# Earlier token transfers, later first weights, and transposing a chunk ahead in a retention and gated-projection kernel

## The chip, the cores and the metric

The kernel runs on one core of one Trainium2 chip. The metric is the device time of one execution in microseconds (us), as the median of several runs. The span of a trace is about 1.8 us shorter than the device time of the same run. All runs told here are of one state, the fast one. TensorE is PE in the profile, VectorE is DVE, ScalarE is ACT, GpSimd is POOL, and SyncE, which issues most transfers, is SP.

## The reference, cut to what matters

A retention block (a linear recurrence over time with a decay for each head) makes x, and x goes through two large products with a gate between them. Inputs are float32, except the two weight matrices, which are float64.

```python
# q, k, v: (4, 8, 768, 64) = batch, heads, time, head size
for t in range(S):
    state = gamma[None, :, None, None] * state + np.einsum('bhd,bhe->bhde', k[:, :, t], v[:, :, t])
    y[:, :, t] = scale * np.einsum('bhd,bhde->bhe', q[:, :, t], state)
# x = y as (3072, 512)
h = x @ w_in                                              # (3072, 2048)
sp = np.maximum(h, 0.0) + np.log1p(np.exp(-np.abs(h)))    # softplus
g = h * erf(sp)
return (g @ w_out).astype(np.float32)                     # (3072, 512)
```

## The kernel before, as far as the argument goes

The kernel takes the time axis in chunks of 128 steps. The first four chunks (0 to 3) of batch 0 make the 512 tokens of the first block. Nothing large can start before these four are through, and no large product can run before its weights are converted. This front of the kernel is what the change rearranges. For each chunk there are six steps:

- `K_` scales q and k by the decays (DVE).
- `T` transposes both on PE, and ACT copies them back.
- `S_` makes the scores on PE.
- `M` applies the causal mask and rescales (DVE).
- `O_` makes the results and the update of the state on PE, and ACT copies the results to `xT`.
- `A` adds the update to the state (DVE).

```python
    for j in range(n_first):          # the first four chunks
        S_(j)
        if j == 0:
            keep_warm(3)              # dummy matmuls
        M(j)
        if j + 1 < n_first:
            K_(j + 1)
        O_(j)
        if j + 1 < n_first:
            T(j + 1)
        ret_loads(j)                  # chunk 3 behind chunk 0; weight pieces
        pace(1)
        if j + 1 < n_first:
            A(j)
```

The weights come in 16 pieces of 1 MB. A piece is converted from float64 to float32 by integer and float operations on DVE, with one square on ACT.

```python
        nc.vector.tensor_scalar(top, hi, 3, 0x3FFFFFF8, ...)           # L205
        nc.vector.scalar_tensor_tensor(top, hi, 0xC0000000, top, ...)  # L209
        nc.scalar.activation(square, square, AF.Square)                # L213
        nc.vector.tensor_scalar(low, top, 0xFF800000, None, ...)       # L215
        nc.vector.scalar_tensor_tensor(lowf, lo, 2.0**-52, lowf, ...)  # L217
        nc.vector.tensor_tensor(lowf, topf, lowf, op=ALU.add)          # L219
        nc.vector.scalar_tensor_tensor(to, square..., lowf...)         # L221
```

These operations are not put behind one another. The build of the program deals them out between the steps of the chunks: `pace(n)` adds n to a counter called `room`, and for every whole unit one conversion operation is emitted. In the traces DVE runs its instructions in the order in which they are emitted.

## Time and profile before

| | before |
|---|---|
| median, lowest, highest of 6 runs | 715.74, 714.52, 718.07 us |
| span of the trace | 714.0 us |
| PE busy, DVE busy | 698.1 us (98%), 398.6 us (56%) |
| first matmul of the first large product | 36.43 us |
| first projection | 70.41 us |

The prediction below shows the main lines of this profile. Two more are needed. They are DVE's operations with the idle time before them in brackets, and what ended it.

```profile
15.36 1.22 DVE L397 TENSOR_TENSOR kq<-kq,kq_s 128x1024 f32<-128x1024 f32 x1 [2.35 <-DMA kq<-in_q_dram]
...
33.28 0.69 DVE L437 TENSOR_TENSOR am<-r,causal 128x512 f32<-128x512 f32 x1 [0.46 <-PE hp L425]
```

The columns are start, duration, engine, line, operation, and output and inputs. The last line is the mask of chunk 3. From there on nothing holds the first block up: its results, then the first large product 3.15 us later.

### The profile page before, as it was taken

How to read it: one execution, taken by the hardware profiler on the slowest of the kernel's cores; microseconds unless marked ns; L12 is line 12 of the kernel's file. 1: busy time of each engine (PE TensorE's matmuls, PEld its weight loads, DVE VectorE, ACT ScalarE, POOL GpSimd, SP SyncE). 2: the span in 40 equal slices, each digit the busy share in tenths (PEclk: the TensorE clock that was granted, in tenths of full speed). 3: DMA queues.
4: the chain of work that ended last, by engine and by line, in shares of the span. 5: the costliest groups of instructions: out<-in, count | busy, mean ns of one | idle time of the engine just before them, and what ended most of it. 6: DMA issues, size and time to landing. Idle time of an engine off the chain costs nothing.

```text
span 714.0 us, 12100 instructions
## 1 busy us (share of the span) xinstructions
PE 698.1 (98%) x5132; PEld 592.4 (83%) x5132; DVE 398.6 (56%) x545; ACT 256.9 (36%) x288; POOL 5.2 (1%) x18
## 2 busy tenths in 40 slices
PE   7899999999999999999999999999999999999996
PEld 6644444486999999999999999989989999999995
DVE  3899999974853553563554454544543553243323
ACT  1345653525144143243242341441441423423440
POOL 1000000010000000000000000000000000000000
PEclk9899999999999999999999999999999999999999
DMA  9999733212321232211222223220311210000000
GB/s 187 214 239 234 176 130 118 39 22 41 100 40 35 70 61 44 58 32 31 61 42 42 66 39 58 65 49 18 69 35 29 45 46 1 1 30 1 1 30 29
DMA packets 147061, 46.96 MB, mean 66 GB/s; under 512 B 135744, under 2 KB 135744, under 8 KB 147008
## 3 DMA queue, kind: packets, MB, share of 16 engines
q1 hardware_dynamic: 143456, 45.40, 29.1%
q10 hardware_dynamic: 3552, 0.80, 0.7%
q8 instruction: 40, 0.66, 0.4%
q14 instruction: 13, 0.11, 0.1%
HBM read 39.86 MB, written 6.29 MB: 65 GB/s over the span
## 4 chain that ended last, share of the span: by engine, by line
PE 93%; ACT 2%; DMA 2%; DVE 2%; issue 1%; ACTq 0%; DVEq 0%
PE hp L607 35%; PE o L664 33%; PE o L550 8%; PE hp L537 7%; PE r L465 3%; PE hp L425 3%; DMA kq<-in_q_dram 2%; PE r L460 1%; PE r L474 1%; PE r L425 1%; ACT e L507 1%; ACT e L506 1%; PE r L412 1%; DMA kq<-in_k_dram 0%; DVE am L437 0%
## 5 line engine op out<-in xcount | busy, mean ns | idle before, releaser
L607 PE MATMUL hp<-xs,w_in_sb 128*128 128x128 f32 x1280 | 149.8, 275 | 0.0
L607 PEld LDWEIGHTS hp<-xs,w_in_sb 128*128 128x128 f32 x1280 | 147.8, 192 | 1.6 <-issue 0.5
L664 PE MATMUL o<-w_out_sb,h 128*128 128x256 f32 x640 | 141.6, 379 | 0.0
L664 PEld LDWEIGHTS o<-w_out_sb,h 128*128 128x128 f32 x640 | 121.6, 190 | 16.5
L526 DVE TENSOR_TENSOR e<-h,e 128x1024 f32<-128x1024 f32 x44 | 51.9, 1221 | 110.9 <-ACT e L507 110.9
L607 PE MATMUL hp<-xT,w_in_sb 128*128 128x128 f32 x960 | 113.7, 275 | 0.0
L607 PEld LDWEIGHTS hp<-xT,w_in_sb 128*128 128x128 f32 x960 | 111.9, 192 | 1.9 <-issue 1.0
L664 PE MATMUL o<-w_out_sb,e 128*128 128x256 f32 x480 | 112.1, 383 | 0.9 <-DVE e L526 0.9
L664 PEld LDWEIGHTS o<-w_out_sb,e 128*128 128x128 f32 x480 | 88.1, 190 | 13.8 <-DVE e L526 1.3
L506 ACT ACT_TABLE_LOAD x24 | 30.8, 1283 | 79.1 <-issue 69.6
L537 PE MATMUL hp<-xT,w_in_sb 128*128 128x512 f32 x128 | 56.9, 596 | 0.5 <-ACT xT L479 0.5
L632 DVE TENSOR_TENSOR h<-h,hp 128x512 f32<-128x512 f32 x20 | 13.7, 687 | 75.3 <-PE hp L607 75.3
L537 PEld LDWEIGHTS hp<-xT,w_in_sb 128*128 128x128 f32 x128 | 23.8, 190 | 28.4 <-issue 27.4
L507 ACT ACTIVATE e<-e 128x2048 f32<-128x2048 f32 x22 | 42.0, 1910 | 0.2
L506 ACT ACTIVATE e<-h 128x2048 f32<-128x2048 f32 x22 | 42.0, 1910 | 0.2
L479 ACT COPY xT<-r 128x256 f32<-128x256 f32 x44 | 14.4, 375 | 74.4 <-PE r L474 65.7
L620 DVE TENSOR_TENSOR h<-h,hp 128x512 f32<-128x512 f32 x20 | 13.7, 687 | 36.5 <-PE hp L607 36.5
L630 ACT COPY h<-hp 128x512 f32<-128x512 f32 x20 | 11.7, 586 | 60.2 <-PE hp L607 60.2
L625 ACT COPY h<-hp 128x512 f32<-128x512 f32 x20 | 11.7, 586 | 57.9 <-PE hp L607 57.9
L623 ACT COPY h<-hp 128x512 f32<-128x512 f32 x20 | 11.7, 586 | 55.3 <-PE hp L607 55.3
L507 ACT ACT_TABLE_LOAD x24 | 30.8, 1283 | 0.4
L627 DVE TENSOR_TENSOR h<-h,hp 128x512 f32<-128x512 f32 x20 | 13.7, 687 | 28.1 <-ACT h L625 28.1
(95 smaller groups left out, 675.5 us busy)
## 6 DMA issues: line engine op xcount, KB each, us to landing
w_out_sb<-in_moe_w_out_dram SPq DMA_DIRECT2D x14, 512.0 KB, 5.0
kq<-in_k_dram SPq DMA_DIRECT2D x24, 256.0 KB, 3.2
v<-in_v_dram SPq DMA_DIRECT2D x24, 256.0 KB, 3.2
w_in_sb<-in_moe_w_in_dram SPq DMA_DIRECT2D x12, 512.0 KB, 7.2
out_dram<-r SPq DMA_DIRECT2D x24, 256.0 KB, 2.3
kq<-in_q_dram SPq DMA_DIRECT2D x256, 16.0 KB, 1.8
kb<-in_k_dram SPq DMA_DIRECT2D x256, 16.0 KB, 1.7
w_out_sb<-in_moe_w_in_dram SPq DMA_DIRECT2D x4, 512.0 KB, 8.4
```

What stands on the lines that cost most here:

```text
L425: nc.tensor.matmul(pp[s][:, hp, :], KT[j][s * D : (s + 1) * D, hp, :], QT[j][s * D : (s + 1) * D, hp, :], start=True, stop=True,)
L465: nc.tensor.matmul(place(h), V[j][:, h, :], AM[j][:, h % 2, h // 2, :], start=(not c and h % 4 < 2), stop=True, skip_group_check=True,)
L479: nc.scalar.copy(XC[m][:, r::2, i * C : (i + 1) * C], pp[r][:, :2, :])
L506: nc.scalar.activation(E[g], HS[g], AF.Softplus)
L507: nc.scalar.activation(E[g], E[g], AF.Erf)
L526: nc.vector.tensor_tensor(E[g][:, half], HS[g][:, half], E[g][:, half], op=ALU.mult)
L537: nc.tensor.matmul(p, w_in_of(ft, kk), XC[0][:, kk, :], start=(kk == 0), stop=(kk == n_k - 1))
L550: nc.tensor.matmul(O[0][tt].rearrange("p (d c) -> p d c", d=2), E[g][:, u * TCH + tt * P : u * TCH + (tt + 1) * P], w_out_of(ft), start=(f ...
L607: nc.tensor.matmul(bank[:, u, :], w_in_sb[:, s, IN[a], kk, u * P : (u + 1) * P], XS[m][b][:, kk, :], start=(p in (1, 2, 5) and u == 0 and ...
L620: nc.vector.tensor_tensor(h["11"], h["11"], flat, op=ALU.add)
L627: nc.vector.tensor_tensor(h["22"], h["22"], other, op=ALU.add)
L664: nc.tensor.matmul(O[m][i][:, half, :], G[g][a][:, u * P : (u + 1) * P], w_out_sb[:, s, OUT[b], u, :], start=i not in started, stop=(s == ...
```

## The change

Its intent is to get the tokens of the first chunks to the engines earlier. The first weight piece is sent behind three chunks instead of behind one, the decays are sent ahead of everything, and for chunks 1 and 2 scaling and transposing are put between the scores and the results of the chunk before. Conversions are held back until chunk 1 is masked (`room` starts at -1000).

```diff
-            queue = nc.scalar if i and j < 3 else nc.sync
+            queue = nc.scalar if i and 0 < j < 3 else nc.sync
...
-    room = 0.0
+    room = -1000.0
...
     nc.scalar.dma_start(d_k, decay_k)
-    load(0)
     ... decays of the state ...
-    load_piece(0)
+    load(0)
     load(1)
     load(2)
-    load_piece(1)
+    load_piece(0)
...
-        if j in (1, 2):
+        if j < 3:
             load_piece(j + 1)
...
     for j in range(n_first):
         S_(j)
-        if j == 0:
-            keep_warm(3)
+        ahead = j < 2
+        if ahead:
+            K_(j + 1)
+            T(j + 1)
         M(j)
-        if j + 1 < n_first:
+        if j == 1:
+            room = 0.0
+        O_(j)
+        if not ahead and j + 1 < n_first:
             K_(j + 1)
-        O_(j)
-        if j + 1 < n_first:
             T(j + 1)
```

The scaling of the decays for the other chunks (`other_scales`) is also emitted earlier in part.

More of the change, by code (lines that the diff above doesn't have):

```diff
@@ L299 @@
     nc.scalar.dma_start(d_k, decay_k)
+    for s in range(2):
+        nc.scalar.dma_start(d_s[:, s], decay_s[s * D : s * D + 1, :].to_broadcast([P, HP]))
     load(0)
     nc.scalar.copy(idle_out, ident[:, :1])
-    for s in range(2):
-        nc.scalar.dma_start(d_s[:, s], decay_s[s * D : s * D + 1, :].to_broadcast([P, HP]))
-    load_piece(0)
     load(1)
     load(2)
-    load_piece(1)
+    load_piece(0)
     causal = const.tile([P, C], F32, name="causal")
@@ L326 @@
     query_scale(0)
+    by = const.tile([P, H], F32, name="by")
+    nc.vector.reciprocal(by.rearrange("p (h s) -> p s h", s=2), d_s)
+    for c in range(1, NC):
+        nc.gpsimd.tensor_tensor(kq_s[:, c, 0], kq_s[:, c - 1, 0], by, op=ALU.mult)
     def other_scales():
-        by = const.tile([P, H], F32, name="by")
-        nc.vector.reciprocal(by.rearrange("p (h s) -> p s h", s=2), d_s)
-        for c in range(1, NC):
-            nc.gpsimd.tensor_tensor(kq_s[:, c, 0], kq_s[:, c - 1, 0], by, op=ALU.mult)
         query_scale(slice(1, NC))
```

## The prediction

> **What bounds the kernel now.** I read the page first, by slices of the span.
>
> ```profile
> PE   7899999999999999999999999999999999999996
> DVE  3899999974853553563554454544543553243323
> PEclk9899999999999999999999999999999999999999
> DMA  9999733212321232211222223220311210000000
> ```
>
> Each digit is a slice of 17.85 us. TensorE (PE) is at 9 from the third slice to the last but one, so everything after about 36 us is bound by TensorE, and nothing in this change alters its work there. What can move is the start: the first two slices, where TensorE has 7 and 8 and a reduced clock, and where DMA is at 9. But VectorE (DVE) is at 9 from the third slice to the seventh: it converts weights there, and TensorE eats them. So a shorter start is only worth what the conversions allow.
>
> Next the busy times of the stages (us, then busy time of PE, weight loads, DVE, ACT, POOL, clock, DMA share, GB/s).
>
> ```profile
> 0.00:18.00 18.00, 12.81 (x107) 11.96 (x108) 6.35 (x12) 3.38 (x7) 2.16 (x13) 0.96 1.05 188
> 18.00:36.00 18.00, 14.84 (x211) 11.84 (x210) 15.50 (x21) 6.49 (x12) 0.00 (x0) 0.85 1.12 214
> 36.00:72.00 36.00, 33.89 (x140) 16.42 (x141) 35.17 (x37) 18.23 (x23) 0.00 (x0) 1.00 1.06 237
> ```
>
> DMA is full at some 190 to 215 GB/s from 2 us on. DVE is idle 11.65 + 2.5 = 14.2 us in the first 36 us and almost never after. TensorE then runs dry only once, by about 1.4 us at 58.7, where it waits for copies on ScalarE (ACT) behind the first softplus and erf.
>
> Then the chain of waits of the first 75 us, which says why the start is slow.
>
> ```profile
> 3.99 11.25 DMA kq<-in_q_dram
> 15.36 1.23 DVE kq L397
> ...
> 36.43 14.02 PE hp L537 x32
> ```
>
> The q of the second chunk is issued at 3.99 and lands only at 15.24, because a megabyte of weights was put in front of it; 15.36 is when the second chunk can be scaled. The first matmul of the big product (L537) starts at 36.43.
>
> Last, where TensorE meets the conversions, from the timelines of DVE and PE.
>
> ```profile
> 16.50 0.69 DVE L205 TENSOR_SCALAR w_out_sb<-w_out_sb 128x1024 uint32<-128x1024 uint32 x1
> ...
> 69.14 1.23 DVE L221 SCALAR_TENSOR_TENSOR w_out_sb<-w_out_sb 128x1024 f32<-128x1024 f32 x1
> ```
> ```profile
> 69.55 1.02 PE L537 MATMUL hp<-xT,w_in_sb 128*128 128x512 f32 x2
> 70.41 13.90 PE L550 MATMUL o<-w_out_sb,e 128*128 128x512 f32 x32
> ```
>
> The weights come in 16 pieces of 1 MB, "in" for the first product and "out" for the projection, of which one projection group needs two. The second "out" piece is ready at 69.14 + 1.23 = 70.37, and the first projection starts at 70.41. In the built program its first matmul waits only for the gating and the piece before; the third of the four matmuls of the first 3.43 us group is the first to wait for this piece, at 70.41 + 1.72 = 72.1. So the conversions have 1.76 us to spare here, no more. The next tight place is the sixth "out" piece, ready at 127.69 + 1.22 = 128.9 against 129.33 + 1.72: 2.1 us.
>
> **What the Trainium skill says.** "DMA: Bandwidth & Descriptors", section "Issuing engines are not separate DMA queues", says that transfers issued from different engines run on the same 16 DMA engines and interleave. The trace agrees in sum: moving a q from ACT's queue to SP's makes no bandwidth. In detail the landings of before follow the order of issue over both queues (k0 4.0, q0 5.5, v0 6.8, the two weight halves 9.8 and 12.4, k1 14.8, q1 15.2, v1 17.2, q2 17.1, k2 18.3, v2 20.5), so I treat them as one line. "TensorE: Matmul & The Clock Gate", section "What's actually happening", says that the clock halves after an idle window and that the window is 3413 ns and runs freely. The trace agrees: TensorE idles from 14.41 to 16.69, the clock reads 0.64 in 16 to 18 us and 0.50 from 18 to 22, and is whole again before 24, some 6.9 us or two windows later. "Perfetto Trace Analysis", section "Optimization Strategy", says that a kernel can have several regimes with different most-contended engines; here they are DMA (to 20 us), DVE (20 to 145) and PE (from 36 on), and the last two overlap.
>
> **The change part by part.**
>
> *Order of the transfers.* The decays go first, then chunks 0, 1, 2, then the first weight piece. The bytes are the same. Chunk 0: k0 and q0 still are the first half megabyte, so q0 lands near 5.4, as before, and the scaling of chunk 0 and its transposes (held by 16 warming matmuls until 7.3 anyway) stay. Its scores end at 10.3, as before. Chunk 1: q1 is behind k0, q0, v0, k1, v1, k2, or 1.05 MB behind v0's 6.8 us; at the 218 GB/s that k, q and v had between 12.4 and 17.2 that is 4.8 us, so 11.6 at the latest, perhaps a little earlier: I take 11.3 in place of 15.2. Chunk 2 is whole by about 14. The first weight piece is then last: 14.0 plus the 5.6 us it took between 6.8 and 12.4 is 19.6, in place of 12.4; before it was not touched until 16.50 though.
>
> *Decays.* Before, the state decay landed at 9.5 and the other scales were ready at 11.8 on DVE. Now they are ready before 8 us. By itself that moves only idle time of DVE; it is needed so that chunk 1 can be scaled early.
>
> *Transposing ahead.* Chunk 1 is scaled (1.22 us, done at 12.5) and transposed between scores and results of chunk 0; the mask of chunk 0 comes after the scaling, 12.5 to 13.8 (two of 0.68) in place of 11.74 to 13.0. Results of chunk 0 then end at 15.4 (half groups of 1.02 and 0.49 us), and scores of chunk 1 follow at once; before, there were 4.9 us between them (14.4 to 19.3). Working on with the same durations: state of chunk 0 16.1 to 16.5, scaling of chunk 2 to 17.6, mask of chunk 1 to 18.9, its results to 21.0, mask of chunk 2 to 24.9, its results to 26.3, scaling of chunk 3 to 27.3, its transposes, copies and scores to 30.3, its mask to 31.6. Before, from the first half mask of chunk 3 (33.28) to the first L537 (36.43) it took 3.15 us; now 30.35 + 3.15 = 33.5. The front gains 2.9 us.
>
> *Conversions.* They start only after the mask of chunk 1 and after the landing at 19.6. DVE's idle time in the front: 2.5 before the decays, 2.2 for q0, 4.1 for q1 (7.2 to 11.3), 2.35 for the results of chunk 0, 0.7 for the weights, 1.55 before the mask of chunk 3 (nothing is put between there now): 13.4 us in place of 13.9 counted gap by gap. So DVE, whose sum of work up to the second "out" piece is the same set of instructions in another order, gains 0.5 us only: the piece is ready at 69.9 less a little, say 69.8.
>
> *The meeting.* TensorE would reach the first projection at 33.5 + 34.0 = 67.5 and need the piece 1.72 later, at 69.2. It waits 0.6 us. Gain 70.41 - 68.1 = 2.3 us. At the sixth "out" piece DVE has 2.1 + 0.5 - 2.3 = 0.3 us left, so it holds. After that TensorE is never short, and the gain stays to the end: 715.5 - 2.3 = 713.2.
>
> **Rivals.** First, *the clock*: three warming matmuls after the first scores are gone, so TensorE now idles from 10.3 to 12.65, as long as the gap of before that halved its clock. If it halves here, transposes of chunk 1 (1.1 us) and results of chunk 0 (1.5) take some 2 us more; DVE waits for both, starts its conversions near 21.4, and is 1.3 us later than before instead of 0.5 earlier. The second piece comes at 71.7, and the gain is 0.5 us: 715.0. For it speaks the equal gap of 2.3 us; against it that the window runs freely, so that a boundary inside the gap saves it. I give it one in two. Second, *the weights take the place of q as the wait*: if the first piece lands at 20.5 (as the same 3.4 MB did before), all of DVE moves back 0.9 us and the gain is 1.4: 714.1. Later landings cost one for one. Third, *nothing comes of it*: DVE, full from 20 to 145 us, gives back all of the front at 70 or 129 us, 715.5. Against that stands the slack of 1.76 and 2.1 us. Fourth, *more than I think*: q1 earlier than 11 gains nothing, since the weight piece still lands at 19.6.
>
> **Range and chances.** Warm with an early piece 713.2, warm with a late one 714.1, cold 715.0 to 715.5. The middle is 713.9. Before scattered from 714.5 to 715.9, so I add 0.7 on either side: 712.3 to 716.1. Two per cent are 14.3 us; DVE and DMA stop TensorE from gaining even 5 us, and the worst case, a cold clock with late weights, loses under 3. Faster by over 2%: 0.01; within 2%: 0.985; slower by over 2%: 0.005.
>
> **What would show it.** Right: the q of chunk 1 is used near 11 to 12, first conversion near 19 to 21, first L537 at 33 to 34.5, the first projection near 68 with a short wait of L550 on DVE (L221) inside its first group, and no further idle time of TensorE. The clock between 12 and 20 us tells the first two cases apart. Wrong: a first L537 earlier than 32 or later than 36, a conversion wait of over 2 us at L550, or a wait at the sixth "out" piece, which would give the gain back.

## The result, and the profile after

| | before | after |
|---|---|---|
| median, lowest, highest of 6 runs | 715.74, 714.52, 718.07 | 714.70, 713.56, 716.21 us |
| span of the trace | 714.0 | 713.2 us |
| PE busy, DVE busy | 698.1, 398.6 | 696.0, 398.7 us |

The ratio is 0.9984, with a 95% interval from 0.9965 to 1.0004: the same time. Ratios here are the mean time of one kernel's fast runs over that of the other's of the same rounds, so they are not quite the ratios of the medians.

First the slices of the page after.

```profile
PE   7698999999999999999999999999999999999996
DVE  4799999984854553563554454544543553243323
PEclk9899999999999999999999999999999999999999
DMA  9999653302322232211222223220311210000000
```

From the fifth slice on the PE row is as before. In the second slice PE fell from 8 to 6 and DVE from 8 to 7, and in the fourth PE fell from 9 to 8. The stages show where (us, then busy time of PE, weight loads, DVE, ACT, POOL, clock, DMA share, GB/s).

```profile
0.00:18.00 18.00, 14.33 (x152) 13.06 (x154) 7.71 (x14) 5.34 (x10) 3.12 (x13) 1.00 1.06 189
18.00:36.00 18.00, 12.23 (x165) 9.55 (x162) 13.36 (x17) 5.23 (x10) 0.00 (x0) 0.81 1.06 208
```

PE and DVE did 1.5 and 1.4 us more in the first 18 us, at full clock, and 2.6 and 2.1 us less in the second 18. DMA is full in both. The chain of waits names what lies between.

```profile
11.56 8.93 DMA w_out_sb<-in_moe_w_in_dram
...
20.58 0.70 DVE w_out_sb L205
...
23.26 0.33 DVE state L494
```

The first weight piece, now last in line, lands at 20.49, and everything of the front hangs on it: the conversions start, and the addition to the state stands behind three of them. Here are DVE's lines.

```profile
9.69 1.23 DVE L398 TENSOR_TENSOR kq<-kq,kq_s 128x1024 f32<-128x1024 f32 x1 [0.54 <-DMA kq<-in_k_dram]
20.58 0.69 DVE L205 TENSOR_SCALAR w_out_sb<-w_out_sb 128x1024 uint32<-128x1024 uint32 x1 [3.80 <-DMA w_out_sb<-in_moe_w_in_dram]
23.18 0.41 DVE L494 TENSOR_TENSOR state<-state,r 128x256 f32<-128x256 f32 x1
31.54 0.69 DVE L438 TENSOR_TENSOR am<-r,causal 128x512 f32<-128x512 f32 x1 [1.89 <-PE hp L426]
70.01 1.23 DVE L221 SCALAR_TENSOR_TENSOR w_out_sb<-w_out_sb 128x1024 f32<-128x1024 f32 x1
```

Chunk 1 is scaled at 9.69 in place of 15.36, so the transfers did what they were meant to. Then DVE waits 3.80 us for the weights. The state addition of chunk 1, at 23.18, needs none of them, but it comes behind L205, L209 and L215 in DVE's order. The mask of chunk 3 is at 31.54 in place of 33.28, that is 1.74 us earlier. But DVE waited 1.89 us for it, where before it had converted.

PE, last, shows both ends of this.

```profile
23.65 0.47 PE L461 MATMUL r<-qT,state 64*64 64x128 f32 x1 [3.57 <-DVE state L494]
...
34.70 17.43 PE L538 MATMUL hp<-xT,w_in_sb 128*128 128x512 f32 x40 [0.47 <-ACT xT L480]
...
68.66 1.88 PE L551 MATMUL o<-w_out_sb,e 128*128 128x512 f32 x4
71.28 12.29 PE L551 MATMUL o<-w_out_sb,e 128*128 128x512 f32 x28 [0.74 <-DVE w_out_sb L221]
83.41 3.60 PE L538 MATMUL hp<-xT,w_in_sb 128*128 128x512 f32 x8
```

PE idles 3.57 us before the results of chunk 2. The first large product starts at 34.70, and the first projection at 68.66, each 1.7 us earlier than before. But the projection stops after four matmuls until DVE has finished the second "out" piece at 70.01 + 1.23 = 71.24. The next product starts at 83.41 in place of 84.15. The lead is down to 0.74 us, and it stays so: the sixth "out" piece's projection starts at 128.59 in place of 129.33.

So the front won 1.74 us and kept 0.74. DVE's books show why. Three conversion operations of the second "in" piece (0.68 + 1.23 + 0.69 = 2.60 us) were done ahead of the mask of chunk 3 before, and come behind it now. The mask is 1.74 us earlier and 2.60 us more are left after it: the second "out" piece is 0.86 us later (71.24 against 70.37), although its work is the same.

The clock explains part of the path in between.

```profile
16.00:20.00 4.00, 4.00 (x71) 3.48 (x69) 0.78 (x2) 1.72 (x4) 0.00 (x0) 1.00 1.18 195
20.00:24.00 4.00, 0.43 (x10) 0.35 (x12) 3.35 (x5) 1.14 (x1) 0.00 (x0) 0.73 0.99 201
24.00:28.00 4.00, 3.39 (x46) 2.69 (x40) 4.00 (x5) 0.00 (x0) 0.00 (x0) 0.50 1.04 217
28.00:32.00 4.00, 3.22 (x48) 2.61 (x44) 2.12 (x4) 1.72 (x4) 0.00 (x0) 0.91 1.06 211
```

The third value from the end is the granted clock: it is halved from about 22 to 28 us, just when PE makes the results of chunk 2. Four matmuls of L466 take 0.64 us there (at 26.46) and 0.39 at full clock (chunk 1, at 17.91).

### The profile page after: what moved, and what is told of

The parts are those of the page before. It is cut to its first block, busy times and chain, and to the rows that moved or that the text cites. A ratio compares the mean times of both kernels' runs of the same rounds, so it can differ in the third digit from the quotient of the medians.

```text
span 713.2 us, 12088 instructions
## 1 busy us (share of the span) xinstructions
PE 696.0 (98%) x5126; PEld 590.8 (83%) x5126; DVE 398.7 (56%) x545; ACT 256.7 (36%) x288; POOL 6.2 (1%) x18
## 4 chain that ended last, share of the span: by engine, by line
PE 89%; DVE 5%; SPq 1%; issue 1%; DMA 1%; ACT 1%; DVEq 0%; ACTq 0%
PE hp L608 35%; PE o L665 33%; PE o L551 8%; PE hp L538 4%; PE r L466 3%; PE hp L426 3%; PE r L461 1%; DMA w_out_sb<-in_moe_w_in_dram 1%; PE r L475 1%; DVE w_out_sb L217 1%; DVE w_out_sb L219 1%; SPq L113 1%; DVE w_out_sb L215 1%; DVE w_out_sb L209 1%; DVE w_in_sb L209 1%
```

## The experiments

Three theories were open. The expectations call them A, B and C, and each says there what it expects of that run. Put shortly, A says that the landing of the first weights sets the conversions, and that these set the end of the front, first of all at the second "out" piece. B says that DVE's order merely changes places, so that a move on one side is given back on another. C says that PE's half clock after its idle time sets it.

Four kernels at a time ran on one chip, beside runs of the kernel before on that chip (medians 716.71, 715.59 and 715.94 us in the three sets). All twelve medians, of fast runs alone, and ratios to before:

| run | median us | ratio | 95% interval |
|---|---|---|---|
| no_ahead | 720.19 | 1.0052 | 1.0029 to 1.0074 |
| weights_early | 720.00 | 1.0048 | 1.0033 to 1.0063 |
| after_skip (wrong result) | 714.82 | 0.9974 | 0.9957 to 0.9990 |
| before_skip (wrong result) | 716.20 | 0.9999 | 0.9979 to 1.0020 |
| chain_first | 725.11 | 1.0130 | 1.0108 to 1.0151 |
| chain_fill | 716.97 | 1.0022 | 1.0005 to 1.0038 |
| warm_fill | 714.93 | 0.9988 | 0.9976 to 1.0001 |
| after_again | 715.11 | 0.9994 | 0.9980 to 1.0008 |
| v2_late | 712.97 | 0.9957 | 0.9942 to 0.9972 |
| v_late | 714.31 | 0.9978 | 0.9963 to 0.9994 |
| v_late_fill | 716.02 | 1.0003 | 0.9988 to 1.0019 |
| weights_later | 716.77 | 1.0012 | 0.9997 to 1.0027 |

### no_ahead: the new order of transfers without transposing ahead

```diff
-        ahead = j < 2
+        ahead = False
+        if j == 0:
+            keep_warm(3)
         if ahead:
```

> The changed kernel with the transposing ahead undone (scaling and transposes of the next chunk after the mask and the results again, three warming matmuls back), the new order of transfers and the late start of the conversions kept. Theory A (the conversions set the gain, and they are held by the landing of the first weights at 20.5): the first conversion still waits for the weights to 20.5, chunk 2 is now scaled behind that wait, so the first L538 falls back to about 36 and the second out piece to about 72; time about 1 us over the changed kernel, no better than before. Theory B (the transfers alone bring the gain, transposing ahead is idle): first L538 at 34.7 and the time of the changed kernel.

It came out 3.5 us slower than before, far more than expected. The trace shows the first conversion at 20.17, as early as in the kernel after, but chunk 2 now stands behind it in DVE's order. PE waits for it, its clock falls, and DVE waits for PE in turn.

```profile
20.17 0.69 DVE L205 TENSOR_SCALAR w_out_sb<-w_out_sb 128x1024 uint32<-128x1024 uint32 x1 [3.00 <-DMA w_out_sb<-in_moe_w_in_dram]
...
37.84 0.69 DVE L438 TENSOR_TENSOR am<-r,causal 128x512 f32<-128x512 f32 x1 [3.42 <-PE hp L426]
```

The mask of chunk 3 is at 37.84 in place of 31.54. Transposing ahead is therefore worth about 5 us once the weights come late (the ratios 1.0052 and 0.9984, of two sets of runs, differ by 0.0068). It does not add to the new order of transfers; it is what makes that order bearable.

### weights_early: the first weights back in their old place, the rest of the change kept

```diff
     load(0)
+    load_piece(0)
     load(1)
     load(2)
-    load_piece(0)
```

> The changed kernel with the first weight piece put back right behind chunk 0; decays first and transposing ahead kept. Theory A: the q of chunk 1 lands near 15 again and the mask of chunk 0, now behind its scaling, ends near 17.7; conversions start near 22, later than with late weights; the second out piece is ready near 72 to 73 and the time is 0.5 to 1.5 us over before. Theory B' (the late weights are the only loss, so early ones would help): conversions start before 20 and the time is 1 us under the changed kernel.

It was 3.3 us slower than before. The wait for the weights is gone, and the wait for the tokens is back.

```profile
16.15 1.22 DVE L398 TENSOR_TENSOR kq<-kq,kq_s 128x1024 f32<-128x1024 f32 x1 [7.12 <-DMA kq<-in_k_dram]
```

PE, with the dummy matmuls gone and chunk 1 missing, was idle for 7.25 us, and its clock read 0.61, 0.50 and 0.61 in the 4 us slices from 12 to 24. The two halves of the change each lose alone (720.0 and 720.2). Only together are they no slower than before. Both runs keep the late start of the conversions (`room` at -1000) and the early decays, which no run tests alone.

### after_skip and before_skip: one addition of the second "out" piece left out

One DVE operation of 1.22 us of just that piece is not done, in either kernel. The result is wrong (relative error 0.35), the timing of the rest is not touched.

```diff
-        nc.vector.tensor_tensor(lowf, topf, lowf, op=ALU.add)
+        if pieces[n] != ("out", 1):
+            nc.vector.tensor_tensor(lowf, topf, lowf, op=ALU.add)
```

> The changed kernel with one VectorE instruction of the second out piece left out (the addition L219, 1.26 us; the result is wrong on purpose). Theory A: the wait of 0.74 us of the projection L551 inside its first group goes, and everything after it comes 0.74 us earlier, first L551 group without a gap; the front (first L538 at 34.7) is as in the changed kernel. Theory C (the halved clock, or something on TensorE, sets the meeting): nothing changes.

> The kernel before with the same one instruction left out (wrong result on purpose). Theory A: there the conversions had 1.76 us to spare, so nothing moves: first L550 at 70.4 and next product at 84.15, time within 0.3 us of before. If conversions already bound the kernel before, it gains 1 us.

In the kernel before nothing changed (0.9999): DVE has room at this place. In the kernel after the wait inside the first projection vanished.

```profile
35.29 17.43 PE L539 MATMUL hp<-xT,w_in_sb 128*128 128x512 f32 x40 [0.47 <-ACT xT L481]
...
69.24 13.90 PE L552 MATMUL o<-w_out_sb,e 128*128 128x512 f32 x32
82.97 3.60 PE L539 MATMUL hp<-xT,w_in_sb 128*128 128x512 f32 x8
```

The pair tells it cleanly. Against the same edit in the kernel before (first large product at 36.26, second at 83.97), this one leads by 0.97 us at the first product and by 1.00 at the second: without the wait for DVE the lead of the front arrives whole. In the kernel after, 1.73 became 0.74. That the wait at L551 takes the rest is shown.

The lead itself was only 0.97 here, though this run's weights were early (first conversion at 19.46). Its clock was at 0.50 from 24 to 32 us, and DVE waited 3.46 us for PE before the mask of chunk 3. This fits a part for the clock, but no run changes the clock alone.

### chain_first: conversions held back for another chunk

```diff
-        if j == 1:
+        if j == 2:
             room = 0.0
```

> The changed kernel with one line moved: conversions may be emitted only after the mask of chunk 2, not after that of chunk 1. The state add of chunk 1 and the mask of chunk 2 then stand ahead of the conversion that waits for the weights at 20.5, so TensorE does not idle 3.6 us for the state add and keeps its full clock from 20 to 28. Theory A (DVE's total of waiting counts, not the front): first L538 at 32 to 33 in place of 34.7, but DVE still stands about 1.9 us before the mask of chunk 3, the second out piece comes only 0.5 us earlier, and the time is at most 0.5 us under the changed kernel. Theory C (the idle TensorE and its halved clock are what costs): the front's 2 us come through in full, projection near 66.5 to 67 without a wait, time 1.5 to 2 us under.

Here the state addition of chunk 1 no longer stands behind conversions. PE kept its full clock from 12 to 40 us, as hoped, and the first large product started at 32.43, another 2.3 us earlier. But it was 1.3% slower than before, and the trace, of the fastest of its five runs (722.61), shows waits for DVE from the first large product on.

```profile
32.43 13.97 PE L538 MATMUL hp<-xT,w_in_sb 128*128 128x512 f32 x32 [2.47 <-DVE w_in_sb L221]
...
66.37 1.88 PE L551 MATMUL o<-w_out_sb,e 128*128 128x512 f32 x4
71.72 13.83 PE L551 MATMUL o<-w_out_sb,e 128*128 128x512 f32 x28 [3.48 <-DVE w_out_sb L221]
```

DVE finished the second "out" piece hardly later than in the kernel after, but PE was 2.3 us earlier and so waited 3.48 us. After that wait its clock was down, and the same 28 matmuls took 13.83 us in place of 12.29. It waited again at 105.80 and 136.07. Neither A nor C had expected this. The later waits have a second cause.

```profile
94.42 1.29 DVE L438 TENSOR_TENSOR am<-r,causal 128x512 f32<-128x512 f32 x2 [4.25 <-PE r L426]
```

DVE, with 53 conversion operations in front of this mask in place of 56, came to it 4.25 us before PE had made the scores; in the kernel after, DVE waits for nothing between 70 and 140 us. So the sixth "out" piece was ready only at 136.02, in place of 129.80. An earlier PE where the conversions are not earlier too cost the first 2 us (next product at 85.39 in place of 83.41); most of the rest is this wait, in which PE's lateness and the missing conversions both have a part. No run moves the state addition alone ahead of the conversions, so what that would bring is open.

### chain_fill: the same, with two conversion operations put before the mask of chunk 3

```diff
+        if j == 3:
+            pace(2)
         M(j)
-        if j == 1:
+        if j == 2:
             room = 0.0
```

> As chain_first, with two more steps of the conversion emitted between scores and mask of chunk 3, where DVE stood idle for 1.9 us. Theory A: the wait before the mask of chunk 3 goes, the second out piece comes near 69, the projection starts near 67.3, and everything after it about 2 us before the changed kernel (3 us before the kernel before). Theory C: nothing over chain_first.

It was the first try at using the 2 us that DVE waits there, and it failed: 716.97 us.

```profile
38.23 1.23 DVE L221 SCALAR_TENSOR_TENSOR w_in_sb<-w_out_sb 128x1024 f32<-128x1024 f32 x1 [2.44 <-ACT w_out_sb L213]
```

The last conversion operation of the piece needs the square, and the square stands in ACT's order behind other work. What DVE gained before the mask, it lost to ACT. PE then waited 3.14 us at the first projection, and its 28 matmuls took 13.98 us, 1.7 more than in the kernel after. The next product came at 84.94, later than before (84.15), although the first had started 3.6 us earlier (32.85). DVE's wait for PE at the mask near 94 us was 1.99 us here, and the loss over the whole run 0.2%: the early start alone does not cost the 1.3% of chain_first.

### warm_fill: eight dummy matmuls in PE's gap

```diff
     for j in range(n_first):
         S_(j)
+        if j == 2:
+            keep_warm(8)
```

> The changed kernel with eight warming matmuls after the scores of chunk 2, where TensorE stands idle from 20.1 to 23.65 and then runs on half clock to some 27. Theory C: clock 1.00 from 20 to 30 in the profile, results of chunk 2 in 1.9 instead of 3 us, mask of chunk 3 about 0.5 us earlier, so 0.5 us off the second out piece and off the time. Theory A says the same 0.5 us and no more, since only the mask of chunk 3 moves on DVE; if the time falls by over 1 us, the clock was the main loss.

The gap before the results of chunk 2 shrank to 2.21 us, and the clock was 1.00 from 20 to 24, but 0.77 and 0.81 in the two slices after: the slow window had moved and not gone. DVE's wait before the mask of chunk 3 was 2.08 us. The time is that of the kernel after (0.9988 against 0.9994 in the same set), so these dummies brought nothing by themselves. As the clock fell all the same, and the weights came late in this run (21.03), that does not rule C out.

### after_again: the kernel after once more

> The changed kernel once more, for the spread: first L538 between 34.2 and 35.5 with the number of slow clock windows, a wait of 0 to 1.5 us inside the first projection group, time 0.5 to 2 us under before.

Its profiled run had the weights earlier by 1.02 us (first conversion at 19.56), and all that follows moved with them, at the same program: mask of chunk 3 at 30.70, the projection's second part at 70.36, the next product at 82.48 in place of 83.41, and a span of 712.3 us in place of 713.2. That gave the idea of the last set: move the landing on purpose.

### v2_late: V of chunk 2 behind the first weights

V of a chunk is needed only for its results, q and k are needed first. 256 KB less are ahead of the weights.

```diff
+        if j == 2:
+            return
+        load_v(j)
+
+    def load_v(j):
...
     load(2)
     load_piece(0)
+    load_v(2)
```

> The kernel after, with V of chunk 2 (256 KB) sent behind the first piece of the first weights instead of ahead of it. Theory A (the landing of the first weight piece sets everything up to the second half of the first projection group, which came 50.7 to 50.8 us after the first conversion in three traces): the piece lands about 1.2 us earlier (first conversion near 19.3 instead of 20 to 20.5), the second half of the first projection group starts near 70.1, time 1 us under the kernel after. Rival C (the half-clock window of TensorE between 20 and 30 us sets it): the first conversion moves and the projection does not; time as the kernel after within 0.3 us.

```profile
18.30 0.69 DVE L212 TENSOR_SCALAR w_out_sb<-w_out_sb 128x1024 uint32<-128x1024 uint32 x1 [1.40 <-DMA w_out_sb<-in_moe_w_in_dram]
29.74 0.69 DVE L446 TENSOR_TENSOR am<-r,causal 128x512 f32<-128x512 f32 x1 [2.37 <-PE hp L434]
```
```profile
33.13 17.43 PE L546 MATMUL hp<-xT,w_in_sb 128*128 128x512 f32 x40 [0.47 <-ACT xT L488]
...
67.08 1.88 PE L559 MATMUL o<-w_out_sb,e 128*128 128x512 f32 x4
69.41 12.29 PE L559 MATMUL o<-w_out_sb,e 128*128 128x512 f32 x28 [0.44 <-DVE w_out_sb L228]
81.53 3.60 PE L546 MATMUL hp<-xT,w_in_sb 128*128 128x512 f32 x8
```

The piece was used 1.26 us earlier than in after_again and 2.28 earlier than in the first trace of the kernel after, and the whole front followed. The median of 712.97 us is 3 us under before, and its interval does not reach 1, so the gain of 0.4% is clear of the noise. It was not run beside the kernel after, but its six times (712.58 to 713.36) all lie under the twelve of that kernel (713.56 at least). Theory A holds in direction; the gain over the kernel after, 1.7 us by the medians, was larger than the 1 us it expected.

### v_late and v_late_fill: V of chunk 3 late as well, and DVE's gap filled

```diff
-        if j == 2:
+        if j in (2, 3):
             return
...
             load_piece(j + 1)
+        if j == 0:
+            load_v(3)
```

and, in v_late_fill alone, `if j == 3: pace(2)` ahead of `M(j)`.

> V of chunks 2 and 3 both behind the pieces of the first weights. Theory A: first conversion 2.4 us earlier than in the kernel after if transfers keep the same rate (near 18), second piece's conversions likewise, second half of the first projection group near 68.5 if the squares and k of chunk 3 don't hold VectorE first; time 1.5 to 2 us under the kernel after. Rival B (VectorE's work on chunks 1 to 3 merely changes places with the conversions, so the second piece's additions end as before): time within 0.5 us of the kernel after, and the wait at the first projection group's second half stays.

> As the run before, and VectorE's two operations of the second piece of the first weights stand ahead of the rescaling of chunk 3 by its masks, to fill the 1.9 us in which VectorE waits there for TensorE. Theory A: second half of the first projection group near 68, no wait on VectorE there, time about 2 us under the kernel after, 3 under the kernel before. Rival B: the gap turns up elsewhere (a wait on ScalarE's square or on the weights' landing), time within 0.5 us of the run before.

For v_late, A was wrong on the landing, by an error of mine: V of chunk 3 had never been ahead of the first weights, since chunk 3 is sent only after chunk 0's results, so nothing ahead of them was taken away beyond v2_late. The first conversion was at 19.65 in this run, and at 18.54 in v_late_fill with the very same order of transfers. So these traces show a landing that varies by a microsecond with nothing changed in the transfers. It also leaves the size of v2_late's gain open: v_late has the same 256 KB taken from ahead of the first weights, and came out at 714.31.

v_late_fill did what it was built for, and lost. The second "out" piece was ready before PE came to it, and the wait at the projection is gone. But conversions were now two operations further ahead everywhere, so two more of them stood before the scaling of chunk 4.

```profile
54.94 5.15 PE L548 MATMUL hp<-xT,w_in_sb 128*128 128x512 f32 x8
...
70.37 13.90 PE L561 MATMUL o<-w_out_sb,e 128*128 128x512 f32 x32
```
```profile
PE r L421 <- DVE kq L406: 3.4, 1, 3.4
```

DVE waited 1.74 us for a later weight piece, which now has more V ahead of it, and scaled chunk 4 at 52.59 in place of 51.03. PE came to its transposes 1.4 us earlier than in v_late and waited 3.4 us for it (the second fence is the list of PE's waits: engine, tile and line, what for, total, times, longest). The clock fell, and eight matmuls took 5.15 us in place of 3.60. The gap had turned up elsewhere, as B expected.

### weights_later: 256 KB of nothing ahead of the first weights

```diff
     load(2)
+    extra = const.tile([P, H, D], F32, name="extra")
+    nc.sync.dma_start(extra, v[0, :, 0:C, :].rearrange("h p d -> p h d"))
     load_piece(0)
```

> The kernel after with a needless transfer of 256 KB ahead of the first weight piece (its result is not used; outputs stay right). Theory A: first conversion 1.2 us later (near 21.5), second half of the first projection group 1.2 us later, time 1.0 to 1.2 us over the kernel after, thus level with the kernel before. Rival C: time within 0.3 us of the kernel after.

The first conversion came at 21.74, 1.16 us later than in the first trace of the kernel after, the projection's second part 2.72 us later (74.00), and the median was 716.77. More than the landing was lost: PE idled 5.36 us before the results of chunk 2, its clock was 0.50 from 24 to 36, and so DVE waited 3.46 us for it before the mask of chunk 3.

### The runs laid side by side

One sum, which is the bookkeeping of DVE's own time, fits the six traces with this order of DVE: second part of the projection = first conversion + 9.07 + wait for PE before the mask of chunk 3 + 39.7. The 9.07 us are DVE's work between the two, the 39.7 us its work from the mask to the end of the second "out" piece.

| run | first conversion | PE idle before results of chunk 2 | DVE's wait before mask of chunk 3 | sum | projection's second part, measured |
|---|---|---|---|---|---|
| v2_late | 18.30 | 1.17 | 2.37 | 69.44 | 69.41 |
| after_again | 19.56 | 2.48 | 2.07 | 70.40 | 70.36 |
| v_late | 19.65 | 2.34 | 2.54 | 70.96 | 71.00 |
| after | 20.58 | 3.57 | 1.89 | 71.24 | 71.28 |
| warm_fill | 21.03 | 2.21 | 2.08 | 71.88 | 71.84 |
| weights_later | 21.74 | 5.36 | 3.46 | 73.97 | 74.00 |

Two terms alone move: the landing, by 3.4 us over these runs, and the wait for PE, by 1.6. The landing is the larger, and in this sum it counts one for one. In all of the six, the state addition of chunk 1 is 2.6 us behind the first conversion, and PE's idle time ends with it, except for the dummies in warm_fill. The wait for PE is what theory C is right about; it does not follow the length of the idle time in order, and no run here has this order with the clock full throughout, so what that would be worth stays open.

## Why the prediction was right or wrong, point by point

The time and the range were right: 713.9 was predicted, 714.70 measured, inside 712.3 to 716.1, and within 2%. This says little for the working: the range held the time of before (715.74) as well, and the middle was an average over rivals. The scatter of before that it took, 714.5 to 715.9, leaves out a run at 718.07. Of the signs that were listed, two were missed: the q of chunk 1 was used at 9.69 and not near 11 to 12, and the first large product started at 34.70, just over 33 to 34.5.

**What bounds it: right.** PE's timeline is a shifted copy from 83.41 on, by 0.74 us.

**Tokens of chunk 1: right in direction, too late in size.** It was to be scaled near 11.3 and was at 9.69. This gained nothing, as the fourth rival had said.

**First weights: the term that was mis-sized first.** The first piece was to land at 19.6, with chunk 2 whole by 14.0 at the 218 GB/s of a stretch of before. That rate held from 2 to 12 us (217 and 219), but in the two slices of 4 us from 12 to 20 it was 196 and 195, and the piece landed at 20.49. In after_again these slices ran at 216 and 205, and the piece was in use at 19.56, so the miss is partly scatter. It is the second rival, "the weights take the place of q as the wait", nearly to the digit, and a later landing did cost one for one or more (weights_later).

**The clock: the rival happened, at another place.** The named gap after the first scores was 0.67 us and not 2.35, as chunk 1 came so early, and the clock was 1.00 through the first 20 us. It halved after the gap before the results of chunk 2. The prediction names no gap there, and its working does not list the state addition of chunk 1, which stood behind three conversions that waited for the weights. Its own times (results of chunk 1 to 21.0, mask of chunk 2 to 24.9) left PE little but 1.2 us of scores to do between.

**The front: right in sign.** The mask of chunk 3 was to be at 30.35 and was at 31.54. Of these 1.19 us the later first conversion (20.58 for 19.6) is 0.98, and DVE's longer wait for PE, 1.89 for 1.55, more than covers the rest. The gain was to be 2.9 us, and was 1.73 at the first large product.

**The conversions: the step that failed.** DVE was to gain 0.5 us up to the second "out" piece and lost 0.87. Gap by gap, DVE idled 14.66 us in the first 36 us in place of the predicted 13.4. The gaps up to chunk 1's scaling are 1.7 us shorter than predicted, but the wait for the weights is 3.80 in place of 0.7. What DVE idles in front of the first conversion is fixed by the landing, however early the tokens come. And the 1.89 us before the mask of chunk 3, where before had only 0.46, were listed in the prediction as 1.55, but not seen for what they are: room for the three operations that now come 2.60 us too late.

**The meeting: right in place and kind.** A short wait of the projection inside its first group was predicted as 0.6 us and was 0.74; the skip runs show that this wait takes the rest of the lead. The sixth "out" piece was to hold by 0.3 us. It was ready at 128.57 + 1.23 = 129.80, and needed at 128.59 + 1.72 = 130.31: it held by 0.5.

**The sum.** 2.3 us warm, 1.4 with late weights and 0.5 with a cold clock were predicted. The traces show 0.74, late weights and a cold clock together; the medians show 1.04, and after_again 0.5 in its set.

## What to carry to other kernels

Here the shared line of transfers was full, so moving one load ahead moved another behind. Ask what will stand at the end of the line and what in each engine's fixed order comes behind its consumer: here it was one small addition behind three conversions. Two engines that meet later, such as converter and consumer, have to gain together; an earlier start of one alone is given back at the meeting, and if the clock falls in the wait there, more than given back (chain_fill: 3.14 us of wait, then 1.7 us of slower matmuls). When a landing sets the path, first look for bytes ahead of it that are needed later: in v2_late, 256 KB moved behind it brought more than the whole change.

## What the Trainium skill lacked or had wrong

- "DMA: Bandwidth & Descriptors", section "Issuing engines are not separate DMA queues", says that transfers of all issuing engines interleave on the same 16 DMA engines. It does not say what a place in the order of issue is worth when they are full: with 256 KB more ahead of them the first weights were in use at 21.74 us (weights_later), and with 256 KB less at 18.30 (v2_late), against 19.56 and 20.58 in the two traces of the kernel after. It also lacks the scatter, which is of the same size: the same order of transfers had the piece in use at 18.54 and 19.65 in two kernels, and at 19.56 and 20.58 in two runs of one.
- "TensorE: Matmul & The Clock Gate", section "What's actually happening", gives the half clock as following at least one idle window of some 3.4 us. In the kernel before, an idle time of 2.28 us was followed by a clock of 0.57 and 0.58 in the two slices of 4 us from 16 to 24; the prediction counted this as agreement. In chain_first, 2.47 us of idle time left it at 1.00. The section's remark that the window runs freely fits the scatter; the length of one gap alone does not decide it.
- The same page, section "A second HAM failure mode: psum-queue depth-cycling", tells of a kernel in which frequent short idle times between groups of matmuls make the clock swing. It does not say how much idle time is enough. v2_late is in line with it: its longest idle time between 18 and 28 us was 1.17 us, PE was busy for 1.61 and 2.25 us of the two slices of 4 us from 20 to 28, and the clock read 0.57 in the slice after.
